# Who issues the loads of attention, where its exponentials stand, and which stores go when: four edits in a chain of attention and two feed-forward layers

## The chip, the cores and the metric

One Trainium2 chip, one of its cores. The metric is the device time of the whole program in microseconds (us), as a median of runs. A run that is profiled gives a trace; its times count from the start of the profiled span. PE is TensorE (matmul), DVE is VectorE, ACT is ScalarE, POOL is GpSimd, SP is SyncE, whose queue issues nearly all DMAs here. "SPq" and "ACTq" in a row mean the issuing of a DMA by that engine.

## The reference

```python
def reference(**kwargs):                       # attention, then two feed-forward layers
    ...
    attn_out = _attn_ref(**attn_kwargs)        # q, k, v: (8, 8, 576, 64), in chunks of 64
    x = np.ascontiguousarray(attn_out.transpose(0, 2, 1, 3)).reshape(B * S, H * D)   # 4608 x 512
    x = _moe_ref(x=x, **moe_kwargs)
    return _moe2_ref(x=x, **moe2_kwargs)

# _attn_ref, chunk by chunk:  scores = scale * q k^T; softmax over a chunk (minus its maximum); times v
# _moe_ref:   h = x @ w_in (512 x 2048);  g = h * clip(h + 3, 0, 6) / 6;  g @ w_out (2048 x 512)
# _moe2_ref:  h = x @ w_in (512 x 1024);  solu = h * softmax(h);  layer norm;  @ w_out (1024 x 512)
```

All of it is float32. A float32 product is made of three matmuls on operands split in a high and a low part (`hi` is a copy rounded by ACT, `lo` the rest, a subtraction on DVE or POOL).

## The kernel before

The 4608 tokens are 36 units of 128, and 9 blocks of 512. Attention works unit by unit (`u`, `NU` = 36) and is spread into the first feed-forward layer of earlier blocks, so that PE has long matmuls while a unit's softmax runs elsewhere. Every engine has its own program order, which is the order of the code (`tc.manual_schedule()`), and each waits for the others by semaphores. So what stands ahead of an instruction on its own engine decides as much as what it depends on.

One unit of attention passes these places:

- `att_slot(w, u)`: PE makes the scores of unit u (`scores`, L398) and the product with v of unit w = u - 1 (`attn_pv` or `attn_pv_raw`, L398 too) in one PSUM tile `att`, of which there is one. ACT copies the product out (L512 or L520). Then come `load_v(w + 2)`, `attn_scores_act(u)` (DVE: maxima L410, scaled L431) and `load_qk(u + 1)`. The tile of q is one, those of k and v are two each. The loads are issued by SP (L129, L130, L136): behind each other, and ahead of whatever SP has to issue next.
- `attn_exp_act(u, heads)`: ACT, eight exponentials (L448), each followed by a read of its accumulated sum.
- `attn_norm(u)`: DVE adds a small number to the sums (L454) and inverts them (L457); POOL or DVE multiplies (L465).
- `attn_turn(u)`: DVE transposes blocks (L490 and four times L494) into `pbd`, which the product with v reads.

The first layer runs in four stages. Block 0 is done unit by unit while the weights arrive. Blocks 1 and 2 are one loop over `F` = 0 to 31, two chunks of 128 of the hidden width for each unit of attention: 12 matmuls `moe_h` (L535), the gate, the split of g, 12 matmuls `moe_o` (L574), and an `att_slot` at odd F. The same loop prepares the weights for Strassen's form (seven products for eight): at each F in `UNITS`, `sums_of` makes sums of two weight chunks (DVE L1052, then four POOL operations L1057 to L1060, in the tiles `tx0`, `tx1` or, for the first three of `w_out`, in `xr0`); two steps later `split_sums` splits them in two halves (ACT L1066, POOL L1067) into four `xo` tiles in turn; `store_sums` issues their stores. `keep_i` and `keep_o` store the plain blocks of `w_in` and `w_out`, 3 and 4 DMAs at a time.

`pair_7(p)` then does two blocks at once, for p = 0 and 1. Its first half is a loop over eight steps j: seven products of 6 matmuls (`mul7`, L1139) named after Strassen's factors. PE's order is A11, S2, S1, the products A22 and S4 of the step before (`finish`), S3, A12, and in six of the eight steps (`event`: all but j = 0 and 5) an `att_slot`. In j = 1, `finish` stands ahead of S1. Around them:

```python
nc.scalar.copy(out=s1, in_=a)                       # L1326, after A11
nc.vector.tensor_add(out=u2, in0=s1, in1=b)         # L1332, after S2; S3 adds to the same b
nc.vector.tensor_add(out=u3, in0=s1, in1=b)         # L1354, after S3
nc.vector.tensor_add(out=c22, in0=u3, in1=c)        # L1356, then two ACT operations and a POOL one
att_slot(u, u + 1)                                  # the end of a step
attn_exp_act(u + 1, range(H))                       # and so ahead of the next step's first copy
```

The second half multiplies by the second weight: seven products i of eight pieces j (`mul_o`, L1276, 6 matmuls each). `prepare(d)` (ACT L1260, DVE L1261, 128x1024 each) splits the operand of two pieces; `prepare(0)` and `prepare(1)` stand behind the loop of the first half, `prepare(2)` behind its last `finish`, the others three ahead of their use. The weights of both halves come through a ring of 16 tiles, each refilled by SP (`ring_fetch`, L1126) once its product is done. `ring_seq` is the list of what it fetches, in PE's order. `pair(2)` does the last two blocks, and the second layer follows.

## Time and profile before

| | before |
|---|---|
| median of 3 runs | 1258.43 us (1256.33 to 1260.02) |
| profiled execution | 1258.94 us, span 1257.1 us |
| PE busy | 1192.2 us (95%) |
| DVE busy | 898.0 us (71%) |
| ACT busy | 722.7 us (57%) |
| POOL busy | 479.5 us (38%) |
| mean granted PE clock | 0.984 of full |

The stages in the trace: block 0 from about 18 to 113 us, blocks 1 and 2 to 315, `pair_7(0)` to 514 (its second half from 421), `pair_7(1)` to 711 (from 618), `pair(2)` to 904, then the second layer.

The profiled execution is 1.8 us longer than its span, and 0.5 us longer than the median. Issuing a DMA is not counted as busy. PE's busy time hides gaps, since matmuls are pipelined and those at a lower clock count as busy too; so PE is read from its waits, row by row, and not from its share. A timeline row gives the start and the duration in us; the bracket at its end is how long the engine stood idle before it and who ended that.

### The profile page before, as it was taken

Reading aid. Unit: us, or ns where it says so; the run is one execution under the profiler, and the core shown is the slowest. Engines: PE = TensorE matmul, PEld = TensorE weight load, DVE = VectorE, ACT = ScalarE, POOL = GpSimd, SP = SyncE. Lnnn points to the kernel's source line nnn. Section 1 sums busy time; section 2 is a strip of 40 time slices with the busy share of each in tenths; the row PEclk is TensorE's granted clock in tenths of the full one; section 3 lists DMA queues with packets and bytes.
Section 4 is the critical chain, followed back from the end, with each engine's and each line's share of the span. In section 5 each row is a group of like instructions: output and inputs, shape, how many; then the busy total and the mean of one; then the engine's idle time right before and its main releaser. Section 6 shows DMA issues by size and latency. Waiting matters only on the chain.

```text
span 1257.1 us, 21419 instructions
## 1 busy us (share of the span) xinstructions
PE 1192.2 (95%) x7199; PEld 964.1 (77%) x7199; DVE 898.0 (71%) x1434; ACT 722.7 (57%) x1655; POOL 479.5 (38%) x560
## 2 busy tenths in 40 slices
PE   8999998999989789998789899999999999999998
PEld 6888776778767578776568778888888888888887
DVE  7887665776566768565676666676988877878774
ACT  7775554554444564244454333354787777867775
POOL 1000564450246400245420011110368667665765
PEclk9999999999999899999899999999999999999999
DMA  9813889642978697686689999885323232222311
GB/s 371 341 51 114 272 277 327 219 136 70 314 254 252 215 358 258 208 266 211 230 297 354 333 342 383 307 302 183 106 68 97 70 98 78 89 90 74 93 59 62
DMA packets 172254, 258.61 MB, mean 206 GB/s; under 512 B 19056, under 2 KB 86896, under 8 KB 172144
## 3 DMA queue, kind: packets, MB, share of 16 engines
q1 hardware_dynamic: 166960, 247.80, 58.2%
q10 hardware_dynamic: 5184, 9.44, 2.0%
q8 instruction: 57, 0.93, 0.3%
q14 instruction: 53, 0.43, 0.1%
HBM read 170.40 MB, written 76.02 MB: 196 GB/s over the span
## 4 chain that ended last, share of the span: by engine, by line
PE 70%; DVE 9%; ACT 7%; issue 6%; POOL 5%; DMA 3%; SPq 0%; POOLq 0%; ACTq 0%; DVEq 0%
PE po L949 16%; PE acc L574 15%; PE hp L535 8%; PE acc L1276 6%; PE hp L1139 6%; PE b L751 5%; PE c L751 3%; PE a L751 3%; ACT p L448 3%; DVE wi L1261 2%; PE att L1139 2%; PE hp L1276 2%; PE acc L1139 1%; PE att L398 1%; DMA xr<-in_moe_w_in 1%
## 5 line engine op out<-in xcount | busy, mean ns | idle before, releaser
L574 PE MATMUL acc<-g_hi,wo 128*128 128x512 f32 x640 | 164.6, 396 | 4.5 <-ACT g_hi L557 4.5
L574 PEld LDWEIGHTS acc<-g_hi,wo 128*128 128x128 f32 x640 | 119.8, 189 | 31.5 <-ACT g_hi L557 5.0
L1139 PE MATMUL acc<-wi,w 128*128 128x512 f32 x420 | 112.9, 419 | 17.4 <-DVE s L1332 16.4
L1139 PE MATMUL hp<-wi,w 128*128 128x512 f32 x468 | 120.0, 400 | 9.4 <-DVE s L1483 3.9
L1139 PEld LDWEIGHTS acc<-wi,w 128*128 128x128 f32 x420 | 83.1, 202 | 39.7 <-DVE s L1332 19.9
L1139 PEld LDWEIGHTS hp<-wi,w 128*128 128x128 f32 x468 | 89.5, 192 | 30.9 <-DVE s L1483 4.4
L1276 PE MATMUL acc<-wi,w 128*128 128x512 f32 x408 | 101.5, 409 | 10.5 <-ACT wi L1260 10.5
L1276 PEld LDWEIGHTS acc<-wi,w 128*128 128x128 f32 x408 | 79.9, 197 | 30.4 <-ACT wi L1260 11.3
L864 ACT COPY wo<-wo 32x256 f32<-32x256 f32 x228 | 92.1, 404 | 18.9 <-DVE wo L846 11.0
L535 PE MATMUL hp<-x_hi,wi 128*128 128x512 f32 x384 | 97.8, 396 | 0.1
L448 ACT ACTIVATE p<-att,mx 128x64 f32<-128x64 f32 x256 | 76.6, 321 | 36.2 <-DVE mx L431 36.2
L1261 DVE TENSOR_TENSOR wi<-wo,wi 128x1024 fp32r<-128x1024 f32 x50 | 66.4, 1347 | 37.8 <-ACT wi L1260 37.4
L732 POOL TENSOR_TENSOR x_lo<-xr,x_hi 128x768 fp32r<-128x768 f32 (+1 forms) x30 | 64.1, 2157 | 75.1 <-ACT x_hi L725 75.1
L574 PE MATMUL acc<-g_lo,wo 128*128 128x512 f32 x320 | 87.6, 390 | 0.0
L535 PEld LDWEIGHTS hp<-x_hi,wi 128*128 128x128 f32 x384 | 71.5, 187 | 17.1 <-ACT x_hi L512 0.3
L836 DVE SCALAR_TENSOR_TENSOR wo<-wo,r,wo 128x1024 f32<-128x1024 f32 x36 | 70.2, 1950 | 1.3
L1260 ACT CAST wi<-wo 128x1024 fp32r<-128x1024 f32 x50 | 51.1, 1070 | 33.5 <-PE hp L1276 15.6
L574 PEld LDWEIGHTS acc<-g_lo,wo 128*128 128x128 f32 x320 | 60.2, 188 | 12.9
L933 POOL TENSOR_TENSOR wo<-wo,wo 128x1024 fp32r<-128x1024 f32 x25 | 63.0, 2518 | 6.2 <-ACT wo L929 3.6
L560 POOL TENSOR_TENSOR g_lo<-t,g_hi 128x512 fp32r<-128x512 f32 x15 | 21.4, 1428 | 106.9 <-ACT g_hi L557 98.9
L541 ACT ACTIVATE t<-hp,three 128x512 f32<-128x512 f32 x48 | 33.3, 693 | 41.3 <-PE hp L535 41.1
L1439 POOL TENSOR_TENSOR s<-s 128x512 f32<-128x512 f32 x4 | 5.1, 1299 | 131.7 <-DVE s L1438 131.7
(318 smaller groups left out, 2883.9 us busy)
## 6 DMA issues: line engine op xcount, KB each, us to landing
w<-sti SPq DMA_DIRECT2D x168, 256.0 KB, 4.4
w<-sto SPq DMA_DIRECT2D x112, 256.0 KB, 4.3
later_t<-xo SPq DMA_DIRECT2D x48, 256.0 KB, 3.8
wo<-later_t SPq DMA_DIRECT2D x24, 512.0 KB, 5.3
wo<-wo SPq DMA_DIRECT2D x328, 32.0 KB, 1.9
x2d<-xo SPq DMA_DIRECT2D x36, 256.0 KB, 4.4
xr<-x2d SPq DMA_DIRECT2D x36, 256.0 KB, 3.4
out<-ob SPq DMA_DIRECT2D x36, 256.0 KB, 2.2
```

What stands on the lines that cost most here:

```text
L448: nc.scalar.activation(out=p_t[u][:, h], in_=sc[:, c, a], func=AF.Exp, scale=0.125, bias=mx[:, m : m + 1], accum_out=sums[u][:, h : h + 1],)
L535: nc.tensor.matmul(hp, wi[f][:, a, kk * P : (kk + 1) * P], b[:, kk], start=(n == 0), stop=(n == 3 * KD - 1),)
L574: nc.tensor.matmul(acc[dc], wo[f][:, w, dc * P : (dc + 1) * P], g[i], start=(at == 0 and n == 0), stop=(at == NF - 1 and n == 2),)
L732: eng.tensor_sub(out=lo[:, f], in0=r, in1=hi[:, f].bitcast(F32))
L751: nc.tensor.matmul(ps, x[:, AT[a], j], w2[w, j][i], start=(start and n == 0), stop=(stop and n == 5), skip_group_check=True,)
L836: nc.vector.scalar_tensor_tensor(out=h, in0=e, scalar=r, in1=h, op0=ALU.mult, op1=ALU.mult, accum_out=mu)
L864: move(out=m[b * 32 : b * 32 + 32, a], in_=tr[a * 32 : a * 32 + 32, b])
L933: eng.tensor_sub(out=lo, in0=m, in1=hi.bitcast(F32))
L949: nc.tensor.matmul(po, a[f], out_w[f][w], start=(n == 0), stop=(n == 3 * NF2 - 1),)
L1139: nc.tensor.matmul(ps, w[:, i, kk * P : (kk + 1) * P], x[:, kk], start=(start and n == 0), stop=(stop and n == 5), skip_group_check=True,)
L1261: nc.vector.tensor_sub(out=e[1], in0=src, in1=e[0].bitcast(F32))
L1276: nc.tensor.matmul(ps[s], w[:, k, s * P : (s + 1) * P], x[l], start=(start and j == 0 and n == 0), stop=(stop and j == NJ - 1 and n == 2), ...
```

## The change

Four edits. (1) `att_slot` has its loads issued by ACT (`nc.scalar`), with those of q and k ahead of `attn_scores_act`. (2) In `pair_7`, the exponentials of a unit move from the end of a step to the next step with an `att_slot`, behind its copy L1326; in the second half they stand at j = 0, and the normalisation and the transposes one piece earlier. (3) `prepare(0)` and `prepare(1)` are issued within the step j = 7; in j = 1 the product S3 stands ahead of S1, and the ring's list follows it. (4) In the loop over F the third unit of `w_out` is summed at F = 7 instead of 9, its split at F = 11 in one go is dropped, and `keep_i`, `keep_o` run at odd F only, over 32 steps instead of 16. No arithmetic is added or removed.

```diff
@@ -121,19 +121,19 @@
     def att_tile(pool, tag):
         return pool.tile([P, DM], F32, tag=tag, name=tag).rearrange("p (h k) -> p h k", h=H)
 
-    def load_qk(u, qt=None, kt=None):
+    def load_qk(u, qt=None, kt=None, eng=nc.sync):
         if u >= NU:
             return
         q_t[u] = att_tile(ap1, "q") if qt is None else qt
         k_t[u] = ks[:, u % 2] if kt is None else kt
-        nc.sync.dma_start(out=q_t[u], in_=q[u])
-        nc.sync.dma_start(out=k_t[u], in_=k[u])
-
-    def load_v(u, vt=None):
+        eng.dma_start(out=q_t[u], in_=q[u])
+        eng.dma_start(out=k_t[u], in_=k[u])
+
+    def load_v(u, vt=None, eng=nc.sync):
         if u >= NU:
             return
         v_t[u] = att_tile(ap2, "v") if vt is None else vt
-        nc.sync.dma_start(out=v_t[u], in_=v[u])
+        eng.dma_start(out=v_t[u], in_=v[u])
 
 
 
@@ -1001,10 +1001,10 @@
             else:
                 attn_pv(w, t, *xn[w // UPB])
             p_t.pop(w, None)
-            load_v(w + 2)
+            load_v(w + 2, eng=nc.scalar)
         if u < NU:
+            load_qk(u + 1, eng=nc.scalar)
             attn_scores_act(u, sc)
-            load_qk(u + 1)
 
     def soft(u):
         attn_exp_act(u, range(H))
@@ -1106,11 +1106,13 @@
         for j in range(NJ):
             ring_seq += inner(j, "A11", "S2")
             if j == 1:
-                ring_seq += inner(0, "A22", "S4")
-            ring_seq += inner(j, "S1")
-            if j > 1:
-                ring_seq += inner(j - 1, "A22", "S4")
-            ring_seq += inner(j, "S3", "A12")
+                ring_seq += inner(0, "A22", "S4") + inner(j, "S3", "S1")
+            else:
+                ring_seq += inner(j, "S1")
+                if j:
+                    ring_seq += inner(j - 1, "A22", "S4")
+                ring_seq += inner(j, "S3")
+            ring_seq += inner(j, "A12")
         ring_seq += inner(NJ - 1, "A22", "S4")
         ring_seq += [("o", n, j) for n, _ in OUTS for j in range(NJ)]
     for j in range(NJ):
@@ -1326,6 +1328,8 @@
             nc.scalar.copy(out=s1, in_=a)
             while todo:
                 todo.pop(0)()
+            if base < u < NU:
+                attn_exp_act(u, range(H))
             b = acc_bank(n + 1) if j else h_psum()
             mul7(b, j, "S2", "T2", True, False)
             u2 = work_tile("s")
@@ -1336,20 +1340,24 @@
                 for g in GROUPS:
                     g_t[g, j // 2] = home(g, j // 2)
             m, k = j // 2, j % 2
-            if late and late[0] == 0:
+            if j == 1:
                 made = finish(*late)
+                mul7(b, j, "S3", "T3", False, False)
             c = h_psum()
             mul7(c, j, "S1", "T1", True, False)
             o_next()
-            if late and late[0] > 0:
+            if j > 1:
                 made = finish(*late)
             if base < u < NU:
                 attn_turn(u)
+            if j == NJ - 1:
+                prepare(0)
             if made:
                 i, t, ps = made
                 gate(t, ps, t)
                 later_sums(i, t)
-            mul7(b, j, "S3", "T3", False, False)
+            if j != 1:
+                mul7(b, j, "S3", "T3", False, False)
             u3 = ap1.tile([P, DM], F32, tag="tx2", name="tx2")
             nc.vector.tensor_add(out=u3, in0=s1, in1=b)
             c22 = g_t["B22", m][:, k]
@@ -1361,13 +1369,12 @@
             t = gp_tile("t")
             ramp(a, t)
             o_next()
+            if j == NJ - 1:
+                prepare(1)
             gate(t, a, g_t["B11", m][:, k])
             if u < NU:
                 att_slot(u, u + 1)
-                attn_exp_act(u + 1, range(H))
             late = j, b, c, s1, u2
-        for d in range(2):
-            prepare(d)
         i, t, ps = finish(*late)
         gate(t, ps, t)
         prepare(2)
@@ -1404,14 +1411,14 @@
                     todo.pop(0)()
                 u = base + 6 + i
                 if i < 3 and u < NU:
-                    if j == 2:
+                    if j == 0:
+                        attn_exp_act(u, range(H))
+                    elif j == 1:
                         attn_norm(u)
-                    elif j == 4:
+                    elif j == 3:
                         attn_turn(u)
                     elif j == 7 and i < 2:
                         att_slot(u, u + 1)
-                        if u + 1 < NU:
-                            attn_exp_act(u + 1, range(H))
                 if final:
                     if (i, j) == (5, 7):
                         second.append(Second())
@@ -1625,7 +1632,7 @@
     STEPS.setdefault(0, []).append(("last", u, (0, 1, 2)))
     STEPS.setdefault(1, []).append(("last", u, (3, 4)))
 
-    UNITS = {2 * j: ("i", j) for j in range(NJ)} | {1 + 4 * j: ("o", j) for j in range(3)}
+    UNITS = {2 * j: ("i", j) for j in range(NJ)} | {1: ("o", 0), 5: ("o", 1), 7: ("o", 2)}
     UNITS |= {2 * j: ("o", j - 5) for j in range(NJ, NJ + 5)}
     todo = None
     for F in range(2 * NF):
@@ -1637,8 +1644,6 @@
         (moe_gate if end else moe_gate_there)(hp, t)
         if F - 2 in UNITS:
             split_sums(*UNITS[F - 2], 1)
-            if F == 11:
-                split_sums(*UNITS[F - 2], 0)
         for step, u, which in STEPS.get(F, []):
             if step == "turn":
                 attn_turn(u, which)
@@ -1657,7 +1662,7 @@
                 if step == "norm":
                     attn_norm(u)
                 attn_turn(u, which)
-        if F - 2 in UNITS and F != 11:
+        if F - 2 in UNITS:
             split_sums(*UNITS[F - 2], 0)
         if F in UNITS:
             sums_of(*UNITS[F])
@@ -1665,10 +1670,8 @@
             soft(NA)
         elif F in (28, 29):
             attn_turn(NA, range(3) if F == 28 else range(3, 5))
-        if F < 8:
-            keep_i(F)
-        elif F < 16:
-            keep_o(F - 8)
+        if F % 2:
+            (keep_i if F < NF else keep_o)(F // 2 % NJ)
         if F == 20:
             todo = prep(0)
         for _ in range(PREP_AT.get(F, 0)):
```

From L1114 on, line numbers of the changed kernel are 2 to 10 higher. ACT's order at a step of `pair_7` (j = 2; `s` is the copy after A11, `p,sm` the exponentials, `xr` and `wi` the copies of the product with v, `t`, `g_hi`, `g_lo` the gates). Before:

```order
L1221 ACTIVATE t<-acc_3819,three 128x512
L520 COPY xr_3924<-att 128x2x2x64
L520 COPY wi_3925<-att 128x2x2x64
L448 ACTIVATE p,sm<-att,mx 128x64 x8
L1326 COPY s<-acc_3962 128x512
L1221 ACTIVATE t<-acc_3830,three 128x512
L1221 ACTIVATE g_hi<-hp,three 128x512
```

Now:

```order
L1223 ACTIVATE t<-acc_3819,three 128x512
L520 COPY xr_3924<-att 128x2x2x64
L520 COPY wi_3925<-att 128x2x2x64
L136 DMA v<-in_v 128x512
L129 DMA q<-in_q 128x512
L130 DMA kbd<-in_k 128x512
L1328 COPY s<-acc_3952 128x512
L448 ACTIVATE p,sm<-att,mx 128x64 x8
L1223 ACTIVATE t<-acc_3830,three 128x512
L1223 ACTIVATE g_hi<-hp,three 128x512
```

The copy and the exponentials have changed places, and three issues of DMAs stand ahead of both.

ACT's order where the first half ends (from the gates of `finish(6)` in j = 7 on; `L1260`, later `L1262`, is the rounding copy of `prepare`). Before:

```order
L1221 ACTIVATE g_hi<-hp,three 128x512
L1221 ACTIVATE g_lo<-wo_4544,three 128x512
L1223 ACTIVATE g_lo<-g_lo,three 128x512
L1221 ACTIVATE t<-acc_4675,three 128x512
L520 COPY xr_4637<-att 128x2x2x64
L520 COPY wi_4638<-att 128x2x2x64
L448 ACTIVATE p,sm<-att,mx 128x64 x8
L1260 CAST wi_4827<-wo_3756 128x1024
L1260 CAST wi_4831<-wo_3987 128x1024
L1221 ACTIVATE t<-acc_4686,three 128x512
L1221 ACTIVATE g_hi<-hp,three 128x512
L1260 CAST wi_4862<-wo_4295 128x1024
```

Now:

```order
L1262 CAST wi_4740<-wo_3756 128x1024
L1223 ACTIVATE g_lo<-wo_4544,three 128x512
L1225 ACTIVATE g_lo<-g_lo,three 128x512
L1223 ACTIVATE t<-acc_4665,three 128x512
L1262 CAST wi_4777<-wo_3987 128x1024
...
L1223 ACTIVATE t<-acc_4686,three 128x512
L1223 ACTIVATE g_hi<-hp,three 128x512
L1262 CAST wi_4852<-wo_4295 128x1024
L1262 CAST wi_4879<-wo_4542 128x1024
L448 ACTIVATE p,sm<-att,mx 128x64 x8
```

Two of the three copies of `prepare` moved ahead of the product with v, and the exponentials moved behind the fourth. DVE's subtractions of `prepare` moved with them: the first stands now between the transposes and the gate of `finish(6)`, the second ahead of the gate of A12.

DVE's order at the end of F = 7 in the loop over blocks 1 and 2 (`pbd` transposes, `hp` the gate of F = 8, `xr` and `tx` the sums of weights). Before:

```order
L490 STREAM_TRANSPOSE pbd<-p 128x512
L494 STREAM_TRANSPOSE pbd<-p 32x8x32 x2
L545 SCALAR_TENSOR_TENSOR hp<-t,hp 128x512
L494 STREAM_TRANSPOSE pbd<-p 32x8x32 x2
L560 TENSOR_TENSOR g_lo<-hp,g_hi 128x512
```

Now:

```order
L490 STREAM_TRANSPOSE pbd<-p 128x512
L494 STREAM_TRANSPOSE pbd<-p 32x8x32 x2
L1052 TENSOR_TENSOR xr_2072<-wo_668 128x512
L1052 TENSOR_TENSOR xr_2072<-wo_727 128x512
L545 SCALAR_TENSOR_TENSOR hp<-t,hp 128x512
L494 STREAM_TRANSPOSE pbd<-p 32x8x32 x2
L560 TENSOR_TENSOR g_lo<-hp,g_hi 128x512
```

The two sums of the third unit of `w_out` stand ahead of the gate of F = 8 now, instead of that of F = 10.

## Rows read from the trace of the kernel before

**Rows 1.** Waits of PE: us in total, times, longest us

```profile
PE acc L1139 <- DVE s L1332: 16.4, 8, 2.1
PE acc L1276 <- ACT wi L1260: 10.5, 2, 5.2
PE att L398 <- DVE pbd L494: 10.1, 15, 2.0
PE att L398 <- ACT p L448: 3.8, 4, 1.5
PE hp L1139 <- DVE s L1483: 3.9, 1, 3.9
```

**Rows 2.** Waits of SP's own queue: us in total, times, longest us

```profile
SPq L136 <- PE att L398: 81.5, 24, 17.0
```

**Rows 3.** Timeline of ACT, from step j = 3 into j = 4

```profile
367.67 0.38 ACT L520 COPY wi<-att 128x256 f32<-128x256 f32 x1
369.56 0.32 ACT L448 ACTIVATE p<-att,mx 128x64 f32<-128x64 f32 x1 [1.51 <-DVE mx L431]
...
371.79 0.24 ACT L448 ACTIVATION_READ_ACCUMULATOR p<-att,mx 128x1 f32 x1
371.89 0.62 ACT L1326 COPY s<-acc 128x512 f32<-128x512 f32 x1
```

**Rows 4.** Timeline of DVE in the same stretch

```profile
372.54 0.69 DVE L1332 TENSOR_TENSOR s<-s,acc 128x512 f32<-128x512 f32 x1 [3.08 <-ACT s L1326]
373.15 0.16 DVE L454 TENSOR_SCALAR sm<-sm 128x8 f32<-128x8 f32 x1
...
376.24 1.80 DVE L494 STREAM_TRANSPOSE pbd<-p 32x256 f32<-32x256 f32 x4
```

**Rows 5.** Timeline of PE, S3 and A12 in two steps of the first half

```profile
358.57 3.03 PE L1139 MATMUL acc<-wi,w 128*128 128x512 f32 x12 [2.08 <-DVE s L1332]
...
373.29 4.62 PE L1139 MATMUL acc<-wi,w 128*128 128x512 f32 x12 [2.14 <-DVE s L1332]
```

**Rows 6.** Timelines of SP and ACT: issuing DMAs

```profile
417.68 0.42 SPq L129 DMA_DIRECT2D q<-in_q  x1
...
752.92 2.75 ACTq L326 DMA_DIRECT2D st<-pbd  x2
```

**Rows 7.** Timelines of PE and DVE in step j = 1

```profile
332.05 1.67 PE L1139 MATMUL hp<-wi,w 128*128 128x512 f32 x6 [1.38 <-DVE wo L1226]
...
335.13 0.69 DVE L1354 TENSOR_TENSOR tx<-s,acc 128x512 f32<-128x512 f32 x1 [2.28 <-PE acc L1139]
```

**Rows 8.** The second half of the first pair: PE, DVE, POOL, and prepare's operations

```profile
425.99 14.25 PE L1276 MATMUL acc<-wi,w 128*128 128x512 f32 x48 [5.23 <-ACT wi L1260]
...
442.83 0.33 PE L398 MATMUL att<-pbd,v 64*64 64x64 f32 x4 [1.97 <-DVE pbd L494]
...
456.70 0.33 PE L398 MATMUL att<-pbd,v 64*64 64x64 f32 x4 [0.44 <-DVE pbd L494]
...
431.28 6.68 DVE L1261 TENSOR_TENSOR wi<-wo,wi 128x1024 fp32r<-128x1024 f32 x3 [0.24 <-ACT wi L1260]
...
432.49 2.16 POOL L1311 TENSOR_TENSOR xo<-wo,wo 128x512 f32<-128x512 f32 x1
...
L1261 DVE TENSOR_TENSOR wi<-wo,wi x50: 1215/1220/2321, 426.0 to 705.9; 128x1024 fp32r<-128x1024 f32 x50
L1260 ACT CAST wi<-wo 128x1024 fp32r<-128x1024 f32 x50 | 51.1, 1070 | 33.5 <-PE hp L1276 15.6 <-PE acc L1276 15.5 <-issue 2.4
```

**Rows 9.** The loop over blocks 1 and 2: PE, ACT and DVE

```profile
170.97 0.69 PE L398 MATMUL att<-kbd,q 64*64 64x64 f32 x32 [1.40 <-ACT p L448]
...
196.38 3.69 PE L574 MATMUL acc<-g_hi,wo 128*128 128x512 f32 x8 [4.54 <-ACT g_hi L557]
...
195.23 0.62 ACT L1066 CAST xo<-xr 128x512 fp32r<-128x512 f32 x1 [7.61 <-DMA sti<-xo]
...
173.79 1.29 DVE L1052 TENSOR_TENSOR tx<-wi 128x512 f32<-128x512 f32 x2 [3.04 <-POOL xo L1067]
```

## The prediction, made before the changed kernel ran

> **What bounds the kernel now.** PE is the engine to shorten, so I read its waits first, summed by who ended them. Most lie in `pair_7`: 16.4 us in eight steps where S3 waits until DVE has read the bank (L1332), 10.5 us at the two starts of the second half, 10.1 us where the product with v waits for DVE's transposes [rows 1]. The loop over blocks 1 and 2 has two kinds: 3.8 us in front of the scores, and one of 4.54 us behind a late g_hi [rows 1, 9]. None of these rows ends in a DMA. SP's own queue stands 81.5 us in front of the loads of v [rows 2], but that is a wait of SP.
>
> Next, the timelines of one step, to see what the eight waits hang on. ACT has copied the product with v by 368.05, waits 1.51 for the maxima, runs the exponentials to 372.03, and only then makes the copy that DVE's L1332 needs [rows 3]. DVE starts L1332 at 372.54, the normalisation at 373.15, ends the transposes at 378.04 [rows 4], and the next product with v can go. So a step with an `att_slot` is a loop through ACT and DVE (transposes, gate, c22, ACT's gates, maxima, exponentials, L1332, normalisation, transposes). PE has slack in it, and its wait at S3 is only where that slack shows first. What a step gains is what this loop loses, not the 2.1 us of the wait.
>
> Waits also slow what follows. After one of 2.08 us twelve matmuls took 3.03 us, after another of 2.14 they took 4.62 [rows 5]; 48 took 14.25 after 5.23 us of idling [rows 8], where 1.4 us for six, which is about the faster pace of [rows 5] without its tail, makes 11.2.
>
> **Loads on ACT.** 84 or so issues leave SP. For PE that is worth nothing: no wait in [rows 1] ends in a DMA, and the cover is the ring's 16 products of lead (16 times 1.4 us), more than SP's longest stop of 17.0 [rows 2]. ACT pays. One issue by SP took 0.42 [rows 6]; two by ACT took 2.75 at the slowest place, so 1.38 each, with whatever they waited for. I take 0.42: q, k and v are free by then, since the copy of the product with v, ahead on ACT, already waited for PE to finish reading them. Behind the issues stand the copy L1326 and the exponentials, or in the loop over F the exponentials alone, and there the wait for the maxima covers them. Without that cover a slot costs 1.3.
>
> **Exponentials behind the copy.** From 368.05: three issues to 369.31, the copy (0.62) to 369.93. The exponentials start there instead of 369.56, 0.37 later, and end at 372.40. L1332 is done by then, so the normalisation starts at about 372.45 instead of 373.15 [rows 3, 4]: 0.7 off the loop, in j = 3, 4 and 7. In j = 2 the maxima come sooner after a copy, and I take 0.4. In j = 5, which has no slot, the copy moves from 371.89 to 369.31 as seen from its step, 2.6 sooner; j = 6 gives back some 0.6, since its exponentials now run between copy and normalisation, and slow matmuls after the wait in front of the product with v, which PE has no slack for there, another 0.8. That leaves 1.2. Sum 0.4 + 3 x 0.7 + 1.2 = 3.7 a pair, **7.4** in all. Bounds: with 1.38 an issue each slot step loses 2.2 instead (a rival, below); with issues hidden altogether it gains 1.1, another 0.4 on four steps of two pairs, 3.2. The eight waits at S3 vanish, and most of them comes back as a longer wait for the transposes L494.
>
> **S3 ahead of S1 in j = 1.** S1 waited 1.38 for the bank of a gate, with S3 behind it; DVE's L1354 waited 2.28 for S3 [rows 7]. Now S3 fills that wait. c22 then hangs on S1, done at 332.05 + 1.67 = 333.7, while before it could start behind L1354, at 335.8: 2.1 a pair, **4.2**. Lower bound is PE's own 1.38, so 2.8.
>
> **First splits within j = 7.** I count from the end of the transposes, DVE's and ACT's 512-wide operations at 0.6 apart [rows 3, 4], `prepare`'s copy at 1.07 and its subtraction at 1.22 (median) or 2.32 (slowest) [rows 8]. DVE: the first subtraction to 1.2, gate, L1354, c22 to 3.0. ACT: two ramps, the ramp of A12, the second copy, to 5.9. DVE: second subtraction to 7.1, gate, maxima, scaling, L1293 to 9.5. ACT: two ramps, third copy to 12.0; DVE's third subtraction to 13.2 or 14.3. PE starts A22 behind L1354 at 2.6, then does two products and four pieces, to 11.0, and waits 2.2 or 3.3 for that third one. So `prepare(2)` is what is late next. The exponentials end near 15.5; normalisation, fifth subtraction and transposes end at 19 or 22, where PE comes at 19.3 or 20.4. PE loses 1.2 before A22, 2.2 or 3.3, 0 or 1.6, and up to 1.5 on slow matmuls: 3.4 or 7.6. Before it lost 5.2, 2.6 (1.97 and 0.6 behind it) and 14.25 - 11.2 = 3.0, that is 10.8 [rows 8]. Gain 7.4 or 3.2. Which price holds: in the kernel before, three of these subtractions in a row took 6.68 while POOL's subtractions beside them took 2.16 [rows 8], and the third subtraction still stands beside the same POOL work (`later_sums`). The Trainium skill says why (SBUF — State Buffer, section "Who interferes with whom"): a DVE instruction with two inputs in SBUF and a GpSimd one that reads SBUF take turns at a shared port pair, and the later one waits for the whole of the other. The trace agrees with 6.68 for three; by this rule the gain is 3.2 a pair, by the median 7.4. The first two subtractions lie where POOL waits, so I take a value nearer the slow end from the rows alone, 4.5 a pair, **9.0**.
>
> The second slot of that half waited 0.44 and some 0.6 for transposes [rows 8]; its exponentials now stand eight pieces of PE ahead of the product with v and its transposes one piece earlier: 1.0 a pair, **2.0**, with 0 as the other end.
>
> **Stores spread, third unit earlier.** The loop over F loses 3.8 + 4.54 [rows 1, 9] and 1.7 on eight matmuls in 3.69 instead of 2.0 (at the pace of [rows 5]), 10.0 together. The 4.54 came from ACT, which stood 7.61 for the store of an `xo` tile [rows 9], at F = 11, where one unit's four tiles were asked for in one go. That goes, since both halves are apart again and `keep` stores half as often: 6.2 gained. Against it: two sums now stand ahead of the gate of F = 8. Alone they take 1.3; with the wait of 3.04 for POOL that such sums have had, 4.3 [rows 9]. POOL has four units in a row to do now, but the tile `xr0` is asked for a step after its last reader, so 2.0, and it falls on the scores of F = 9, which waited 1.40 already. At F = 11 the same two sums no longer stand ahead, 0.8 back. Net **5.0**; ends 1.9 - 1.0 = 0.9 (4.3, and another wait of 1.0 from POOL) and 10.0 (all of it gone).
>
> **Sum.** 7.4 + 4.2 + 9.0 + 2.0 + 5.0 = 27.6. The profiled execution took 1258.9, so 1231.3; it stood 0.5 above the median of the runs shown, so I say 1231. Measurement tells some 0.3% (3.8 us) from no change.
>
> **Rivals.**
> *Waits only move* (12%): the loop through ACT and DVE does not get shorter, because issues cost 0.7 and eat the gain. For it: ACT's gap is 1.51 [rows 3] and three issues and a copy fill it to the brim. Then 7.4 and 2.0 go: 1241.
> *POOL bounds the loop over F* (12%): four units in a row, each wait of DVE for POOL grows beyond 3.04 [rows 9], the gain is near 0: 1236.
> *More* (14%): the subtractions run at 1.22, and stores land so soon that no wait in the loop over F is left: another 2 x 2.9 and 5: 1220.
> *ACT is held by its issues* (5%): 1.38 each as in [rows 6], 4.1 a slot. The exponentials come 2.9 later than by my count in each of 14 slots in `pair_7`: 1231 + 40 = 1271, slower. It decides from 27.6 / 14 / 3 = 0.66 above my price, at 1.1 us an issue. Against it: the issues have nothing to wait for.
> *Wait at the start of `pair(2)`* (2%): 3.9 now [rows 1], behind loads of the next weights; if those come no sooner while PE comes 20 us sooner, it doubles: 1235.
>
> My forecast, 1226 to 1236, has 52%. Faster in all but the fourth and a few per cent for what I have not seen: faster 0.93, same 0.03, slower 0.04. The range leaves out the fourth and the edges of the first and third: 1219 to 1243.
>
> **What would show it.** Right: no wait of PE for L1332 in `pair_7` from j = 2 on; the wait for L494 there 2 to 3 us in one piece; steps with a slot 14.0 us apart instead of 14.7; the start of the second half waiting not at its first but at its fifth piece, some 3 us; no wait of 4.5 in the loop over F, but 3 us in front of the scores of F = 9. Wrong: issues on ACT more than 0.6 us apart, exponentials starting a microsecond behind the maxima, PE waits that end in a DMA of q, k, v or of the ring, or POOL without a gap from F = 6 to 11.

## The result and the profile after

| | before | after |
|---|---|---|
| median | 1259.22 us (1256.33 to 1261.78) | 1228.06 us (1227.03 to 1229.14) |
| span of the profiled execution | 1257.1 us | 1225.2 us |
| mean granted PE clock | 0.984 | 0.986 |

The ratio is 0.9753, 95% interval 0.9729 to 0.9778: 31.2 us less, where 27.6 were forecast. The time lies inside the range, 3 us below the point. The terms of the sum fared much worse than the sum.

The waits of PE in the changed kernel, summed by who ended them (us in total, times, longest). Line numbers are two to eight higher: L1261 is now L1263, L1332 is L1336, L1354 and L1356 are L1362 and L1364.

```profile
PE att L398 <- DVE pbd L494: 18.1, 19, 1.9
PE acc L1141 <- DVE tx L1362: 3.3, 2, 1.8
PE hp L1141 <- DVE s L1490: 3.0, 1, 3.0
PE att L398 <- ACT p L448: 2.8, 1, 2.8
PE acc L1278 <- DVE wi L1263: 1.9, 2, 1.2
...
PE acc L398 <- DMA wo<-in_k: 1.4, 2, 1.1
```

Against [rows 1], the 16.4 us of S3 behind L1332 are gone, the 10.5 for ACT's cast at the starts of the second half have become 1.9 for DVE's L1263, and the wait for the transposes L494 has grown from 10.1 to 18.1. A wait for the transposes is where a loop through ACT and DVE shows when nothing on PE's side shows it sooner. So these sums tell that the place of the wait moved; how much time left, they don't tell. For that I measure the distance from the end of one product with v to the end of the next, in PE's timeline. For p = 0, with four of the experiments below (one profiled execution each):

| us, p = 0 | before | after | exps_at_end | splits_behind | both_reordered | pool_held |
|---|---|---|---|---|---|---|
| j = 2 | 11.84 | 11.59 | 11.89 | 11.59 | 12.10 | 11.59 |
| j = 3 | 14.65 | 13.57 | 14.64 | 13.57 | 12.32 | 11.62 |
| j = 4 | 14.94 | 13.65 | 14.87 | 13.62 | 12.39 | 11.60 |
| j = 5 and 6 | 23.41 | 21.44 | 25.04 | 21.47 | 21.28 | 21.21 |
| j = 7 | 14.83 | 13.56 | 14.64 | 13.56 | 12.34 | 11.61 |
| start of the second half | 27.20 | 23.61 | 26.79 | 23.47 | 22.49 | 18.05 |
| its second slot | 13.87 | 13.87 | 13.88 | 13.91 | 14.54 | 14.42 |

The stages, from the first matmul of one to that of the next: the loop over F 201.2 to 195.1 us, `pair_7(0)` 197.9 to 187.0, `pair_7(1)` 197.7 to 184.8, `pair(2)` with the second layer 546.1 to 543.4. The gain lies where the prediction put it, in `pair_7` and the loop over F.

The timeline of one step of the changed kernel (start, duration; in brackets the idle time ahead and who ended it), ACT, then DVE, then PE:

```profile
358.05 0.72 ACT L1225 ACTIVATE g_lo<-g_lo,three 128x512 f32<-128x512 f32 x1
358.06 0.33 ACTq L136 DMA_DIRECT2D v<-in_v  x1
358.49 0.39 ACTq L129 DMA_DIRECT2D q<-in_q  x1
358.68 0.67 ACT L1223 ACTIVATE t<-acc,three 128x512 f32<-128x512 f32 x1
358.97 0.39 ACTq L130 DMA_DIRECT2D kbd<-in_k  x1
359.25 0.36 ACT L520 COPY xr<-att 128x256 f32<-128x256 f32 x1
...
359.76 0.61 ACT L1328 COPY s<-acc 128x512 f32<-128x512 f32 x1
361.39 0.31 ACT L448 ACTIVATE p<-att,mx 128x64 f32<-128x64 f32 x1 [1.02 <-DVE mx L431]
...
359.38 0.69 DVE L1228 SCALAR_TENSOR_TENSOR wo<-t,acc 128x512 f32<-128x512 f32 x1 [2.18 <-ACT t L1223]
...
363.90 0.17 DVE L454 TENSOR_SCALAR sm<-sm 128x8 f32<-128x8 f32 x1 [2.01 <-ACT p L448]
...
367.93 0.33 PE L398 MATMUL att<-pbd,v 64*64 64x64 f32 x4 [1.58 <-DVE pbd L494]
```

The reader is to see three things. The issues of v, q and k (ACTq) run from 358.06 to 359.36, *while* ACT executes the ramps, and each starts ahead of the copies of the product with v, which stand before them in program order: ACT's sequencer hands work over faster than ACT does it, and here it has time for the issues. The copy L1328 follows the copies at once, 0.40 us after the last issue has ended. And the exponentials still wait 1.02 us for the maxima, so the copy in front of them costs them nothing: j = 3 and 4 got 1.08 and 1.29 us shorter, where I had left 0.7. The row of 2.18 on DVE matters further down.

### The profile page after: what moved, and what is told of

Same layout as the page of the kernel before. It is cut to its first block, busy times and chain, and to the rows that moved or that the text cites. A ratio compares the mean times of both kernels' runs of the same rounds, so it can differ in the third digit from the quotient of the medians.

```text
span 1225.2 us, 21435 instructions
## 1 busy us (share of the span) xinstructions
PE 1186.6 (97%) x7199; PEld 963.1 (79%) x7199; DVE 901.6 (74%) x1434; ACT 721.7 (59%) x1655; POOL 477.5 (39%) x560
## 4 chain that ended last, share of the span: by engine, by line
PE 77%; DVE 7%; issue 5%; ACT 4%; POOL 4%; DMA 2%; ACTq 1%; SPq 0%; POOLq 0%; DVEq 0%
PE acc L574 16%; PE po L949 16%; PE hp L535 9%; PE acc L1278 7%; PE hp L1141 6%; PE b L751 5%; PE hp L1278 4%; PE c L751 4%; PE a L751 4%; PE att L1141 2%; ACT p L448 2%; PE att L398 2%; PE acc L1141 1%; PE att L751 1%; DVE wi L1263 1%
## 5 line engine op out<-in xcount | busy, mean ns | idle before, releaser
L1141 PE MATMUL acc<-wi,w 128*128 128x512 f32 x420 | 108.7, 407 | 3.3 <-DVE tx L1362 3.3
L1278 PE MATMUL acc<-wi,w 128*128 128x512 f32 x408 | 96.1, 393 | 1.9 <-DVE wi L1263 1.9
L1141 PEld LDWEIGHTS acc<-wi,w 128*128 128x128 f32 x420 | 80.7, 195 | 21.6 <-DVE tx L1362 3.6
L1278 PEld LDWEIGHTS acc<-wi,w 128*128 128x128 f32 x408 | 76.6, 189 | 19.6 <-DVE wi L1263 2.8
L1263 DVE TENSOR_TENSOR wi<-wo,wi 128x1024 fp32r<-128x1024 f32 x50 | 65.8, 1333 | 28.7 <-ACT wi L1262 28.2
L836 DVE SCALAR_TENSOR_TENSOR wo<-wo,r,wo 128x1024 f32<-128x1024 f32 x36 | 73.9, 2053 | 1.3
L1262 ACT CAST wi<-wo 128x1024 fp32r<-128x1024 f32 x50 | 51.5, 1066 | 32.6 <-PE hp L1278 15.8
```

The costliest lines, as they stand in the source:

```text
L836: nc.vector.scalar_tensor_tensor(out=h, in0=e, scalar=r, in1=h, op0=ALU.mult, op1=ALU.mult, accum_out=mu)
L1141: nc.tensor.matmul(ps, w[:, i, kk * P : (kk + 1) * P], x[:, kk], start=(start and n == 0), stop=(stop and n == 5), skip_group_check=True,)
L1263: nc.vector.tensor_sub(out=e[1], in0=src, in1=e[0].bitcast(F32))
L1278: nc.tensor.matmul(ps[s], w[:, k, s * P : (s + 1) * P], x[l], start=(start and j == 0 and n == 0), stop=(stop and j == NJ - 1 and n == 2), ...
```

## Experiments

Each edit is of the changed kernel unless its text says otherwise; each was run in five rounds beside the kernel before, and the ratios are to that. The changed kernel's ratio of 0.9753 is the one to compare with.

**exps_at_end**

```diff
-            if base < u < NU:                       # behind the copy L1328
-                attn_exp_act(u, range(H))
...
                 att_slot(u, u + 1)
+                attn_exp_act(u + 1, range(H))
```

and the second half's places as before.

> The changed kernel with the exponentials back at the end of a step, and with the second half's order of before; the loads stay on ACT. By the prediction's sum this costs 7.4 + 2.0 = 9.4: 1237.5. By what the traces show of the two loops (a step with a slot 13.6 us long instead of 14.7, in three or four steps of a pair, j = 5 and 6 together 2.0 shorter) it costs 10 to 13: 1238 to 1241, with L1332's kind of wait (u2, DVE, ahead of S3) back in eight steps of some 2 us. By the rival that waits only move it costs 0 to 2: 1228 to 1230.

Measured: 1247.07 us, ratio 0.9900 (0.9883 to 0.9916). That is 19.0 more, twice the prediction's price and more than the second theory too. Its PE waits and one stretch of PE's timeline:

```profile
PE acc L1141 <- DVE s L1334: 16.2, 8, 2.1
PE att L398 <- DVE pbd L494: 9.5, 14, 3.3
```

```profile
426.37 0.97 PE L1278 MATMUL acc<-wi,w 128*128 128x512 f32 x2 [3.42 <-ACT wi L1262]
428.62 7.61 PE L1278 MATMUL acc<-wi,w 128*128 128x512 f32 x22 [1.28 <-DVE wi L1263]
```

The eight waits of S3 are back, and the steps are those of before (third column of numbers in the table; for j = 5 and 6 the two pairs change places, 25.0 and 23.4 us here, 23.4 and 25.2 before). In PE's timeline the steps lose 12.4 us in the two pairs. What neither side had expected is the start of the second half: 26.79 and 27.21 us, about as before and 7.0 in all above the changed kernel, though the first splits are still issued within j = 7. The exponentials behind `att_slot` stand on ACT ahead of the ramps of the last `finish` and of the cast of `prepare(2)`, and PE waits 3.42 for that cast.

**splits_behind**

```diff
-            if j == NJ - 1:
-                prepare(0)
...
-            if j == NJ - 1:
-                prepare(1)
...
+        for d in range(2):
+            prepare(d)
         i, t, ps = finish(*late)
```

> The changed kernel with prepare(0) and prepare(1) behind the loop of the first half. The prediction put these at 9.0 for two pairs (ends 6.4 and 14.8): 1237 (1234 to 1243). The start of the second half was 23.6 us from the end of one product with v to the end of the next in the changed kernel and 27.15 in the kernel before, 3.5 a pair; with the exponentials now ahead of the first piece, part of this may be their doing, so I expect 5 to 8: 1233 to 1236, with a wait of PE at the first piece of 3 to 5 us. If the subtractions beside POOL cost as much as they bring: 1228 to 1230.

Measured: 1228.26 us, ratio 0.9762 (0.9742 to 0.9783): nothing. PE and DVE at its start of the second half:

```profile
411.34 5.78 PE L1278 MATMUL acc<-wi,w 128*128 128x512 f32 x24 [1.35 <-DVE wi L1263]
...
425.52 0.33 PE L398 MATMUL att<-pbd,v 64*64 64x64 f32 x4 [1.95 <-DVE pbd L494]
...
415.38 4.45 DVE L1263 TENSOR_TENSOR wi<-wo,wi 128x1024 fp32r<-128x1024 f32 x2 [0.25 <-ACT wi L1262]
419.75 1.27 DVE L454 TENSOR_SCALAR sm<-sm 128x8 f32<-128x8 f32 x1
```

PE waits at other pieces than in the changed kernel (there 1.77 ahead of A22 and 0.68 at the fifth piece), but the product with v waits for the transposes in both, 1.95 here and 1.92 there. The two subtractions of 4.45 us start 12.5 us after the end of the transposes before them, against 12.6 in the changed kernel, so the early splits brought nothing to the chain through DVE that sets the end. PE's waits ahead of it are that chain's slack. With exps_at_end this says that the gain at the start of the second half is the exponentials', and the next run shows it directly.

**exps_alone**: the edit of exps_at_end the other way, as the only one in the kernel *before*.

> The kernel before with one edit: the exponentials behind a step's first copy, and in the second half at j = 0 with normalisation and transposes one piece earlier; loads on SP, all else as before. The prediction's sum for this is 9.4: 1249. Theory from the undone edit (19 us lost without it): 17 to 21 gained, 1238 to 1242, of it some 7 at the two starts of the second half. If it needs the loads on ACT or the early first splits beside it: 5 to 10 gained, 1249 to 1254.

Measured: 1238.29 us, ratio 0.9830 (0.9810 to 0.9850), 20.7 less than the 1259.0 beside it. Its starts of the second half are 23.35 and 23.62 us long, as in the changed kernel (23.61 and 23.35). Two thirds of the whole gain come from where a unit's eight exponentials stand, and they need neither the loads on ACT nor the splits.

**loads_on_sp**

```diff
-            load_v(w + 2, eng=nc.scalar)
+            load_v(w + 2)
         if u < NU:
-            load_qk(u + 1, eng=nc.scalar)
             attn_scores_act(u, sc)
+            load_qk(u + 1)
```

> The changed kernel with q, k and v issued by SP again, q and k behind the maxima. Theory: the issues cost ACT nothing where it is busy and gained PE nothing: 1226 to 1230, and SP stands some 80 us again in front of the loads of v. Rival 1: SP's stops kept the ring or the next weights late, and their going is part of the gain: 3 to 8 us more, with waits of PE for a DMA, at the start of pair(2) above all (0.4 of a DMA wait now, 1.9 before). Rival 2: the issues do hold up ACT: 3 to 6 us less.

Measured: 1227.95 us, ratio 0.9752 (0.9733 to 0.9771): no difference. Its waits of SP's queue show how little such a wait says:

```profile
SPq L136 <- PE att L398: 100.6, 28, 17.0
```

SP stands 100.6 us in front of the loads of v, more than in [rows 2], and PE loses nothing by it.

**twice_the_issues**: the loads on ACT in two halves each.

```diff
+                eng.dma_start(out=d[:64], in_=s[:64])
+                eng.dma_start(out=d[64:], in_=s[64:])
```

> Each load of q, k and v by ACT as two DMAs of 64 partitions: three more issues a slot, nothing else. If ACT's sequencer issues them while ACT still works off operations that it was handed before, three more of 0.4 are mostly covered by the gate's ramps and by the 1.0 us in which ACT waits for the maxima: 0 to 3 us more, 1228 to 1231. If an issue takes 0.42 of ACT's own time, as the prediction priced it, six stand in front of the copy, the exponentials of a slot in pair_7 start 1.2 to 1.5 later, and 14 slots cost 17 to 21: 1245 to 1249.

Measured: 1269.15 us, ratio 1.0084 (1.0058 to 1.0110): 41 more than the changed kernel, past both expectations. One slot of it on ACT:

```profile
373.72 0.55 ACTq L131 DMA_DIRECT2D q<-in_q  x1
373.89 0.38 ACT L528 COPY wi<-att 128x256 f32<-128x256 f32 x1
374.32 0.61 ACTq L132 DMA_DIRECT2D q<-in_q  x1
377.43 0.49 ACTq L131 DMA_DIRECT2D kbd<-in_k  x1
377.97 0.61 ACTq L132 DMA_DIRECT2D kbd<-in_k  x1
378.62 0.58 ACT L1336 COPY s<-acc 128x512 f32<-128x512 f32 x1 [4.35 <-DMA q<-in_q]
```

ACT has finished its copies at 374.27, and the copy L1336 comes 4.35 later. Two things hold it: the halves take 0.47 to 0.61 an issue instead of 0.33 to 0.44 (medians), and k's first half is issued 2.5 us after q's second, by the profile behind a DMA of q. The copy starts 0.04 us after the last issue has ended. So the rival *ACT is held by its issues* is a real mechanism: what stands behind an issue in ACT's program waits for it. My theory that issues are simply hidden fell; they are hidden as long as ACT still has earlier work to do. Three issues left 0.40 us to spare in the step shown above, and six here took longer than that work. The run did more than double a cost, since it also brought a wait for a DMA, and why that wait is there was not tried.

**f_loop_undone** and **units_undone**: the edits of the loop over F undone, all of them, or without the spread stores.

```diff
-    UNITS = ... | {1: ("o", 0), 5: ("o", 1), 7: ("o", 2)}
+    UNITS = ... | {1 + 4 * j: ("o", j) for j in range(3)}   # 1, 5, 9; the split at F == 11 in one go
...
-        if F % 2:                                            # f_loop_undone only
-            (keep_i if F < NF else keep_o)(F // 2 % NJ)
+        if F < 8: ...                                        # as before: keep_i, then keep_o
```

> The changed kernel with all edits of the loop over F undone (the third unit of w_out at F = 9 with its split at F = 11 in one go, keep_i and keep_o at each of F = 0 to 15). The prediction put them at 5.0 (ends 0.9 and 10); the loop was 6.1 shorter in the changed kernel's trace. Expected: 5 to 7 more, 1233 to 1235, with the wait of some 4.5 us behind a late g_hi back and the wait in front of the scores of F = 9 gone or near 1.4. Rival: the 4.5 went because the loads left SP's queue, so that the stores of xo land sooner: then 1228 to 1230 and no such wait.

> The changed kernel with the third unit of w_out at F = 9 again and its split at F = 11 in one go, but keep_i and keep_o at odd F over 32 steps. If spreading the stores took the 4.5 us away and the early unit brought the wait of 2.75 at F = 9: some 3 us less than the changed kernel, 1224 to 1226, with neither wait. If the burst of F = 11 made the 4.5: 1231 to 1234, with that wait back and the wait at F = 9 near 1.4.

Measured: 1233.10 us, ratio 0.9788 (0.9775 to 0.9801), and 1233.27 us, ratio 0.9792 (0.9775 to 0.9810). The edits are worth 5.0 and 5.2 (in PE's timeline the loop is 4.8 and 5.8 longer), and the spread stores none of it. In f_loop_undone the wait behind a late g_hi is back with 2.03 us instead of the 4.5 expected, and a wait for a load of k comes beside it:

```profile
193.73 2.50 PE L574 MATMUL acc<-g_hi,wo 128*128 128x512 f32 x8 [2.03 <-ACT g_hi L557]
...
202.93 0.69 PE L398 MATMUL att<-kbd,q 64*64 64x64 f32 x32 [1.80 <-DMA kbd<-in_k]
```

ACT stood 5.14 us for a store of an `xo` tile there, and the issue of that load stands behind this stop in ACT's program. The kernel before has the same burst with the loads on SP, and no wait of PE for k; so I put the late load down to ACT's stop. The changed kernel's loop shows no such wait. What the loop's edits are worth with the loads on SP was not tried. In units_undone the stop at F = 11 looks like this on ACT and PE:

```profile
190.40 0.62 ACT L1066 CAST xo<-xr 128x512 fp32r<-128x512 f32 x1 [2.45 <-DMA sti<-xo]
195.73 0.37 ACT L520 COPY xr<-att 128x256 f32<-128x256 f32 x1 [4.22 <-POOL xo L1067]
...
202.52 1.13 PE L398 MATMUL att<-kbd,q 64*64 64x64 f32 x32 [4.79 <-ACT p L448]
```

The burst of four `xo` tiles stops ACT (2.45 for a store, and 4.22 until POOL's L1067 had read the tile `xr`, which ACT's copy then writes), and PE loses 4.79 in front of scores. In the changed kernel that is gone, and the early unit costs the wait forecast at F = 9:

```profile
172.49 0.72 PE L398 MATMUL att<-kbd,q 64*64 64x64 f32 x32 [2.75 <-ACT p L448]
...
174.00 3.23 PE L574 MATMUL acc<-g_hi,wo 128*128 128x512 f32 x8
```

From product to product that slot is 15.62 us, against 13.84 in units_undone; the one at F = 13 is 12.40 against 18.06, the one at F = 15 12.40 against 14.39.

**s1_first**: `mul7(b, j, "S3", ...)` of j = 1 back behind S1, in the ring's list too.

> The changed kernel with the order of j = 1 as before (S1 ahead of S3, in the list of the ring too). The prediction put this at 2.1 a pair, 4.2 in all: 1232. If only PE's own wait of 1.38 counts, 2.8: 1231. If the loop through ACT and DVE, now shorter, catches up in j = 2: 1228 to 1229.

Measured: 1230.39 us, ratio 0.9761 (0.9747 to 0.9775), 2.3 more. That is within the intervals of the two ratios, so it is PE's timeline that shows it: the step j = 1 is 1.39 and 1.36 us longer, which is PE's own wait, the lower bound, and j = 2 does not catch up (11.59 in both).

What holds the loop now? Two rows gave the next experiments: DVE stands 2.18 a step for the ramp of A12, queued on ACT behind two ramps of c22 though its product was long done; and the start of the second half hangs on DVE.

**start_reordered** and **both_reordered**

```diff
+            if hang:                              # both_reordered: behind the next exponentials
+                ramp(*hang, True)
...
-            t = gp_tile("g_lo")
-            ramp(c22, t, True)
-            nc.gpsimd.tensor_mul(out=c22, in0=t, in1=c22)
             mul7(a, j, "A12", "B21", False, True)
             t = gp_tile("t")
             ramp(a, t)
+            w = gp_tile("g_lo")
+            hang = c22, w
...
             if j == NJ - 1:
-                prepare(1)
+                rest.append(cast(1))              # ACT's copy alone; cast(0) in place of prepare(0)
+                if u < NU:
+                    att_slot(u, u + 1)
...                                               # c22's ramps, then the exponentials
             gate(t, a, g_t["B11", m][:, k])
+            if j == NJ - 1:
+                while rest:
+                    rest.pop(0)()                 # both subtractions
```

This is both_reordered; start_reordered has only the part at j = 7, with c22's ramps behind A12 in the other steps and ahead of the ramp of A12.

> The changed kernel with another order at the end of j = 7: ACT's copies of prepare(0) and prepare(1) and the ramp of A12 ahead of the ramp of c22, the slot's maxima ahead of the last gate, the exponentials behind the slot, both subtractions behind c22. Theory: the start of the second half is bound by the chain of ACT and DVE from one unit's transposes to the next one's, so exponentials that start some 6 us sooner shorten it: 23.6 us from product to product become 17 to 20, so 7 to 13 less in two pairs: 1215 to 1221. Rival: PE waits for the subtractions beside POOL instead, as in the changed kernel: 1225 to 1230.

> The kernel start_reordered, and in each step ACT's ramp of A12 ahead of that of c22, which goes behind the next exponentials. DVE stood 2.18 us in each step for the ramp of A12, which stands behind two ramps of c22 on ACT and whose product was done before. Theory: the loop of ACT and DVE gets 1.5 to 2.2 shorter in j = 3, 4 and 7 and in j = 5 with 6, to PE's own 11.6 or so a step: another 6 to 16 less in two pairs than start_reordered: 1201 to 1214. Rival: POOL's later work or PE's slow matmuls set the pace at once: as start_reordered, within 3.

Measured: 1227.18 us, ratio 0.9732 (0.9714 to 0.9751), and 1216.64 us, ratio 0.9655 (0.9641 to 0.9668). The ramp's order gives the steps of 12.3 us in the table and 10.5 us in all, inside the 6 to 16 expected of it, though the steps did not reach 11.6 and the time is above 1201 to 1214, since start_reordered had missed its own range. At the start of the second half start_reordered gained 1.1 and 1.7 us in the two pairs, where 3.6 to 6.6 were expected, and the rival was right: exponentials that start sooner help little as long as DVE's subtractions stand beside POOL's.

**pool_held**: of both_reordered, with POOL's subtractions of j = 7 behind an instruction that has to wait.

```diff
         prepare(2)
+        prepare(3)
+        if base + 6 < NU:
+            attn_norm(base + 6, nc.gpsimd)
+        nc.gpsimd.tensor_mul(out=c22, in0=w, in1=c22)
         later_sums(i, t)
...                                               # in the loop, POOL's product for c22 behind the
                                                  # normalisation; the first slot's steps earlier
```

> The kernel both_reordered with POOL held back at the start of the second half: prepare(3) and the normalisation stand ahead of POOL's product for c22 and of its four subtractions of j = 7, with the normalisation's product on POOL, and the transposes of the first slot two pieces earlier; in the loop POOL's product for c22 goes behind the normalisation. Theory: DVE's subtractions of prepare (2.1 to 2.2 us each beside POOL, 1.2 alone), its 1.26 and its 1.5 us for the normalisation are what holds the start; then 22.3 us from product to product become 18 to 19, and 6 to 9 go in two pairs: 1208 to 1211. Rival: POOL's work only moves on to the next subtractions and the second slot gives it back: 1214 to 1218.

Measured: 1209.20 us, ratio 0.9597 (0.9578 to 0.9615). The stretch of the start in both_reordered, DVE and POOL, and then the same one in pool_held, with a product with v in one of its steps:

```profile
411.10 4.43 DVE L1263 TENSOR_TENSOR wi<-wo,wi 128x1024 fp32r<-128x1024 f32 x2 [0.25 <-ACT wi L1262]
415.45 1.26 DVE L454 TENSOR_SCALAR sm<-sm 128x8 f32<-128x8 f32 x1
...
414.53 2.16 POOL L1327 TENSOR_TENSOR xo<-xo,wo 128x512 f32<-128x512 f32 x1
```

```profile
408.70 2.36 DVE L1263 TENSOR_TENSOR wi<-wo,wi 128x1024 fp32r<-128x1024 f32 x2 [0.25 <-ACT wi L1262]
410.97 0.17 DVE L454 TENSOR_SCALAR sm<-sm 128x8 f32<-128x8 f32 x1
...
411.52 1.04 POOL L465 TENSOR_TENSOR p<-p,sm 128x512 f32<-128x512 f32 x1 [6.87 <-ACT wi L1262]
...
364.18 0.28 PE L398 MATMUL att<-pbd,v 64*64 64x64 f32 x4
364.83 0.68 PE L398 MATMUL att<-pbd,v 64*64 64x64 f32 x28 [0.36 <-DVE pbd L494]
```

While POOL stands idle for 6.87 us, two subtractions take 2.36 instead of 4.43 and the small addition 0.17 instead of 1.26. The start of the second half is 18.05 us long, inside the 18 to 19 expected, and a step 11.6, which is PE's own work but for 0.36.

The edit does more than hold POOL back, and it does not keep all that it gains. Of the 4.4 us at the start, these rows account for 2.07 and 1.09; most of the rest is the product of the normalisation, 1.50 on DVE before and on POOL now, and a subtraction of 1.21 that no longer stands ahead of the transposes, against a wait of 1.22 for POOL. And for p = 1 the second slot is 14.43 us long where it was 11.83, with PE waiting 0.52 for a subtraction and 1.04, by the profile, for a DMA: there the rival was right. For p = 0 it is 14.42 against 14.54, but in both_reordered's execution 48 matmuls of it took 13.52 us, with a granted clock of 0.50 from 424 to 428 us.

**pool_held_sp**: of pool_held, with the edit of loads_on_sp.

> The kernel pool_held with q, k and v issued by SP again, q and k behind the maxima. In pool_held ACT's queue is empty when a slot's issues come, so that they are seen: the first copy of a step starts 0.3 behind the last issue and 0.93 behind ACT's last work. But PE now sets the pace of a step (11.6 us, its own work), so that even so the issues should cost nothing: 1207 to 1211. If the issues on ACT do cost where they are seen, 2 to 5 less: 1204 to 1207. If the loads off SP are what lets the ring keep up with a faster PE: 3 to 10 more, with waits of PE for a DMA.

Measured: 1209.54 us, ratio 0.9587 (0.9569 to 0.9606): no difference here either. But the premise of the expectation was a misreading. The first copy of a step in pool_held, and then in pool_held_sp, where the loads are SP's:

```profile
354.82 0.44 ACTq L130 DMA_DIRECT2D kbd<-in_k  x1
355.53 0.59 ACT L1341 COPY s<-acc 128x512 f32<-128x512 f32 x1 [0.93 <-PE acc L1141]
```

```profile
356.84 0.59 ACT L1341 COPY s<-acc 128x512 f32<-128x512 f32 x1 [0.93 <-PE acc L1141]
```

The copy waits 0.93 for PE's A11 in both, and the issues are over 0.27 before it starts. So three issues hold up nothing in these steps either; only twice_the_issues shows what happens when they do. Edit 1 is not needed for the fastest version found, which is some 50 us below the kernel before with it or without.

## Why the prediction was right, term by term

| term | said | undone, or done alone |
|---|---|---|
| exponentials, with the second slot | 7.4 + 2.0 | 19.0 undone, 20.7 alone |
| S3 ahead of S1 | 4.2 | 2.3 (2.75 in PE's timeline) |
| first splits within j = 7 | 9.0 | 0.2 |
| loop over F | 5.0 | 5.0 |
| loads on ACT | 0 | -0.1 |
| sum | 27.6 | 26.4, of 31.2 measured |

**The time was right by luck: two errors cancelled.** The step that failed is "First splits within j = 7", put at 9.0 and worth 0.2; the exponentials, put at 9.4 with the second slot and worth 19.0, made up for it. The gain at the start of the second half is there, 3.6 and 3.8 us (4.5 forecast), but I credited it to the splits, since I compared the start of before with one that has *all* edits and priced only the splits. Counted as I did, from the end of the transposes, the next ones were to end at 19 or 22 us, with PE there at 19.3 or 20.4. In the changed kernel they end at 23.6, and PE is there at 20.8. DVE shows why:

```profile
416.40 4.44 DVE L1263 TENSOR_TENSOR wi<-wo,wi 128x1024 fp32r<-128x1024 f32 x2 [0.25 <-ACT wi L1262]
420.77 1.27 DVE L454 TENSOR_SCALAR sm<-sm 128x8 f32<-128x8 f32 x1
...
422.31 1.51 DVE L465 TENSOR_TENSOR p<-p,sm 128x512 f32<-128x512 f32 x1
```

The exponentials are done at 419.6, 15.8 us by that count where I had 15.5. But after two slow subtractions the addition and the product of the normalisation take 1.27 and 1.51 as well, where the same two took 0.17 (pool_held) and 0.69 (the kernel before) without POOL beside them. This chain ends last, and an earlier wait of PE moves nothing as long as it does.

**Exponentials.** The mechanism was right: L1332's wait gone from j = 2 on, L494's grown, one loop through ACT and DVE. The size was not: steps of j = 3, 4 and 7 lost 0.9 to 1.3 us instead of 0.7, because I put 1.26 us of issues in front of the copy, and they cost ACT nothing there. In j = 5 and 6 it was 2.0 and 3.8 instead of 1.2. The forecast of steps 14.0 us apart was wrong by that: they are 13.6. And 7.0 of the 19.0 are the starts of the second half, which I had put down to the splits. At the second slot the waits of 0.44 and 0.59 for p = 0 did go, but in the changed kernel's execution the 48 matmuls ahead of it took 12.85 us instead of 11.27, so that its 13.87 us stayed; in loads_on_sp and exps_alone, with 11.3 for them, it is 12.3.

**S3 ahead of S1.** c22 does come 2.1 us sooner, as forecast, but in j = 1 PE is not behind that chain, and only its own 1.38 counts.

**The shared port.** The price of 2.2 held (4.44 for two in the changed kernel, with POOL's beside them at 2.15). The Trainium skill's rule (SBUF — State Buffer, section "Who interferes with whom": the two engines take turns at a shared port pair) agrees with 2.36 and 4.43 for the same two subtractions without and with POOL. The addition of eight columns has one tensor input, and still took 1.26: in both_reordered it ended at 416.71, POOL's subtraction beside it at 416.69. The same section allows for that, since it counts operations with a scalar among those that can take both ports under certain conditions; whether this one did, no run shows.

**Loop over F.** Right in its sum; inside it, spreading the stores brought nothing, the earlier unit and the end of the burst, which no run parts, did it all, and the wait at F = 9 was 2.75 where 1.40 and 2.0 made 3.4.

**Rivals.** *Waits only move* fell with steps of 13.6 us. *ACT is held by its issues* was excluded for three issues by loads_on_sp, and came about with six. *POOL bounds the loop over F* and *Wait at the start of `pair(2)`* did not come: no such wait of PE in the first, and 3.0 and 0.4 in the second where there were 3.9 and 1.9. *More* came at neither of its two places: subtractions beside POOL still took 2.2, and the loop over F kept a wait of 2.75.

**Signs.** Of those named beforehand, S3's wait for L1332 is gone from j = 2 on, and so is the one of 4.5 in the loop over F, with 2.75 in front of the scores of F = 9. Issues on ACT are 0.6 us apart or less in `pair_7`, but for two (1.37 and 0.97), whose steps are no longer than the others. Two did not come: no wait for L494 is longer than 1.9 in one piece (2 to 3 forecast; a step's wait comes in two, 1.58 and 0.59), and at the fifth piece of the second half PE waits 0.68 instead of some 3, which points at the step that failed.

**Open.** 4.8 of the 31.2 us belong to no single edit; each term is a difference of two medians whose intervals are 1.6 to 3.1 us to either side. Two places scatter by as much from one execution to the next: the second wait at the start of `pair(2)`, for ACT's L319, was 1.9 before, 0.4 after and 0.4 to 2.7 in the experiments; and the loop over F took 2.1 us more in the trace of exps_alone than in that of before, with the same code there. Whether edits help each other by the rest wasn't tried.

## What to carry to other kernels

When engines wait for each other in a loop, price an edit by the distance between two passes of the loop, with all other edits held fixed; the total of a wait only says where the loop's slack shows. Look in an in-order queue for an operation that is ready and stands behind one that is not: the ramp of A12 (10 us) and the exponentials (20 us) were both that. And an engine off the path can still set the pace by a shared port: held back behind an instruction that has to wait, it lets the other engine's operations run shorter (2.36 us for 4.43 here), as long as its own work does not come back where it is needed next. Last, before crediting a gain to an edit, ask which chain ends last at that place: the early splits shortened one that did not.

## What the hardware showed that was not expected

The same 48 matmuls at the second slot took 12.85 us in the changed kernel and 11.28 in loads_on_sp. The waits just ahead of them were the same (1.92 and 0.59; 1.94 and 0.59), and so nearly was PE's busy time in the two windows ahead (0.63 and 0.86 us of 2; 0.60 and 0.86). The windows of the changed kernel (length; PE, PEld (weight loads), DVE, ACT, POOL busy, each with its count of instructions; granted clock, DMA share, GB/s), and then one of loads_on_sp:

```profile
428.00:430.00 2.00, 2.00 (x14) 1.53 (x9) 2.00 (x3) 1.10 (x3) 0.00 (x0) 0.76 1.02 388
430.00:432.00 2.00, 2.00 (x6) 1.59 (x5) 0.98 (x3) 2.00 (x7) 0.00 (x0) 0.50 0.97 353
432.00:434.00 2.00, 2.00 (x9) 1.61 (x9) 0.85 (x2) 2.00 (x15) 0.00 (x0) 0.89 0.92 325
```

```profile
430.00:432.00 2.00, 2.00 (x10) 1.63 (x9) 1.78 (x3) 2.00 (x10) 0.00 (x0) 1.00 1.01 380
```

The clock stood at its lower level, 1.2 GHz, for a stretch around 430 to 432 in one and at 2.4 throughout in the other. So the slow matmuls behind a wait, which the prediction counted as part of each wait's price, are granted or not by something that this wait alone doesn't set, and a term for them carries an uncertainty of some 1.5 us a place.
